# Threshold attention into a squared-ReLU feed-forward: the first batch in two parts, a maximum per head, and the sums' transposes between the value products

## The chip, the cores and the metric

The kernel runs on one NeuronCore of a Trainium2 chip. The metric is device microseconds of one execution. Every execution listed here was fast: within 1.5% of the fastest of its kernel. Where a run was timed against the kernel before, both ran alternately on the same chip. Different jobs ran on different chips, and the kernel before then had medians of 1672.2 to 1674.6 us; so kernels of different jobs are compared by their ratios to it. A ratio is the mean time of one kernel's fast runs over that of the other's in the same rounds, so it is not quite the ratio of the medians quoted.

## The reference

```python
batch, n_heads, seq, head_dim = (8, 8, 576, 64)      # q, k, v; float32
scores = (1 / sqrt(64)) * q @ k.T
thresh = max(scores) - tau                            # tau = 0.02
scores = where(scores >= thresh, scores, -1e9)
attn   = exp(scores - max(scores)); attn /= sum(attn) + 1e-9
x = (attn @ v) as (4608 tokens, 512)
out = relu(x @ w_in) ** 2 @ w_out                     # w_in 512 x 2048, w_out 2048 x 512
```

The weights come as float64. The kernel reads each number as two 32-bit words and makes a float32 of them.

## The kernel before

Two heads are handled together (a pair). A batch has four pairs. Queries go in five blocks per pair: four of 128 rows and one of 64, in which both heads share the partitions. So a batch has 20 blocks, called slots here, and eight batches have 160. All instructions on TensorE stand in the order in which the program emits them; on the other engines a scheduler orders them when the program is built. DVE, ACT and GpSimd take their instructions strictly in that order, as the Trainium skill's page "TensorE: Matmul & The Clock Gate" says (Part 1, on queue depths).

One slot: scores on TensorE into PSUM, softmax on DVE and ACT, transposes of the weights `w` on TensorE.

```python
def softmax(i, t, sc):                       # (cut)
    every = ...                              # both heads, 2 x 576 columns
    nc.vector.tensor_reduce(out=nmx[:, 0:nj], in_=every, axis=AXIS.X, op=ALU.max, negate=True)
    nc.vector.tensor_scalar(out=thr[:, 0:nj], in0=nmx[:, 0:nj], ...)
    for j in range(nj):
        nc.scalar.activation(out=w[:, ts(j, S)], in_=sc[...], func=AF.Exp, bias=nmx[:, j : j + 1])
    for j in range(nj):
        nc.vector.scalar_tensor_tensor(out=w[...], in0=sc[...], scalar=thr[:, j : j + 1], in1=w[...],
            op0=ALU.is_ge, op1=ALU.mult, accum_out=sm[...])
```

After a pair's five blocks come its value products. From the second batch on, the transposes of the reciprocal sums stand behind the products:

```python
    pv = [bank([P, n], "pv") for _, n in parts]          # 512 and 64 queries
    ...                                                  # products of v with the weights
    if b > 0:
        reciprocals()     # transposes pr, copy rb on ACT, transpose prr, copies rb on ACT
    for (q0, n), to in zip(parts, pv):
        ...  nc.vector.tensor_mul(xs[piece][...], to[...], rb[...])
```

The four banks of `bank()` (two in the first batch) serve all of these, the transposes and the feed-forward. A piece of feed-forward is 256 tokens: 64 products with `w_in` (out `ph`), 32 with `w_out` (out `po`). Its matmuls are put between the scores and the transposes of later slots, so that TensorE has work while softmax runs. In the first batch there are no finished tokens yet, so there is nothing to put in.

The weights are converted from the first slot on, 1.25 of 32 chunks per slot; in the trace 27 fall in the first batch and 5 in the second. One chunk passes through three engines:

```python
    nc.scalar.activation(out=a, in_=hi, func=AF.Abs)                            # L120
    nc.gpsimd.tensor_scalar(out=a, in0=a, ..., op0=ALU.min, op1=ALU.max)        # L122, the clamp
    nc.vector.tensor_scalar(out=t, in0=a, ..., shift and mask)                  # L126
    nc.vector.scalar_tensor_tensor(out=t, in0=hi, ..., in1=t)                   # L130
    nc.scalar.activation(out=r, in_=lo, func=AF.Copy, scale=2.0**-29)           # L134
    nc.gpsimd.tensor_tensor(out=dst, in0=t, in1=r, op=ALU.add)                  # L135
```

## Time and profile before

The median is 1674.5 us (1674.1 to 1674.6).

| stretch (us) | what runs | TensorE busy | granted clock | DVE busy | ACT busy |
|---|---|---|---|---|---|
| 9 to 136 | first batch, no feed-forward | 78% | 0.79 | 74% | 68% |
| 136 to 322 | second batch and feed-forward | 99% | 0.99 | 39% | 39% |
| 322 to 1502 | six batches and feed-forward | 99% | 1.00 | 34% | 35% |
| 1502 to 1673 | feed-forward alone | 97% | 1.00 | 1% | 11% |

A busy TensorE at a clock of 0.79 does less in the same time: both columns have to be read together. The conversion, which becomes important below, is seen in the groups of instructions with the shapes kept apart (line, engine, operation, shapes and count, then busy us and mean ns, then idle time of the engine before them and what ended it):

```profile
L126 DVE TENSOR_SCALAR t<-a 128x512 int32<-128x512 int32 x32 | 17.7, 554 | 22.3 <-POOL a L122 22.3
```

DVE stood 22.3 us for GpSimd's clamp in the whole run.

```profile
DVE t L126 <- POOL a L122: 7.7, 9, 2.6
```

### The profile page before, as it was taken

How to read it: one execution, taken by the hardware profiler on the slowest of the kernel's cores; microseconds unless marked ns; L12 is line 12 of the kernel's file. 1: busy time of each engine (PE TensorE's matmuls, PEld its weight loads, DVE VectorE, ACT ScalarE, POOL GpSimd, SP SyncE). 2: the span in 40 equal slices, each digit the busy share in tenths (PEclk: the TensorE clock that was granted, in tenths of full speed). 3: DMA queues.
4: the chain of work that ended last, by engine and by line, in shares of the span. 5: the costliest groups of instructions: out<-in, count | busy, mean ns of one | idle time of the engine just before them, and what ended most of it. 6: DMA issues, size and time to landing. Idle time of an engine off the chain costs nothing.

```text
span 1673.3 us, 19432 instructions
## 1 busy us (share of the span) xinstructions
PE 1616.4 (97%) x7616; PEld 1034.6 (62%) x7616; DVE 568.9 (34%) x1210; ACT 589.0 (35%) x1237; POOL 255.5 (15%) x296
## 2 busy tenths in 40 slices
PE   6879999999999999999999999999999999999998
PEld 3446666575756566575666665758575665756764
DVE  5784433333433333322223233333333333320000
ACT  5774433343433333332323333334333333321100
POOL 3451201020101101010110110102010110102211
PEclk7888999999999999999999999999999999999999
DMA  6551110101010010100000001010110000000000
GB/s 170 157 172 41 35 34 22 34 16 32 23 28 21 21 28 22 34 15 20 23 27 20 22 22 34 22 29 21 28 28 20 23 21 13 1 13 7 7 13 13
DMA packets 98347, 55.79 MB, mean 33 GB/s; under 512 B 83664, under 2 KB 91856, under 8 KB 98256
## 3 DMA queue, kind: packets, MB, share of 16 engines
q1 hardware_dynamic: 95376, 45.11, 10.3%
q0 software_dynamic: 2880, 9.44, 1.5%
q8 instruction: 61, 1.00, 0.2%
q14 instruction: 30, 0.25, 0.0%
HBM read 45.09 MB, written 9.44 MB: 33 GB/s over the span
## 4 chain that ended last, share of the span: by engine, by line
PE 91%; issue 3%; ACT 2%; DVE 2%; POOL 1%; DMA 1%; SPq 1%; POOLq 0%; ACTq 0%
PE ph L367 30%; PE po L382 29%; PE sc L233 11%; PE pv L343 7%; PE pwT L284 6%; PE pqk L194 2%; PE pv L337 2%; PE pr L324 1%; ACT rb L325 1%; PE pwR L294 1%; PE pwT L289 1%; DVE w L263 1%; DMA raw<-in_moe_w_in_dram 1%; ACT w L259 1%; DVE t L130 0%
## 5 line engine op out<-in xcount | busy, mean ns | idle before, releaser
L367 PE MATMUL ph<-x,w_in 128*128 128x256 f32 x2304 | 515.9, 381 | 5.1 <-ACT rb L325 5.1
L382 PE MATMUL po<-w_out,g 128*128 128x512 f32 x1152 | 512.3, 597 | 7.9 <-ACT rb L325 7.9
L367 PEld LDWEIGHTS ph<-x,w_in 128*128 128x128 f32 x2304 | 432.2, 190 | 69.4 <-ACT rb L325 7.3
L251 DVE TENSOR_REDUCE nmx<-sc 128x2 f32<-128x1152 f32 (+1 forms) x160 | 197.9, 1237 | 688.8 <-PE sc L233 677.4
L382 PEld LDWEIGHTS po<-w_out,g 128*128 128x128 f32 x1152 | 213.2, 190 | 254.5 <-issue 240.1
L263 DVE SCALAR_TENSOR_TENSOR w<-sc,thr,w 128x576 f32<-128x576 f32 x288 | 225.0, 815 | 134.8 <-ACT w L259 134.8
L259 ACT ACTIVATE w<-sc,nmx 128x576 f32<-128x576 f32 x288 | 200.0, 743 | 148.1 <-DVE nmx L251 146.6
L285 ACT COPY wT<-pwT 128x512 f32<-128x512 f32 x256 | 138.4, 589 | 316.5 <-PE pwT L284 316.3
L375 POOL TENSOR_TENSOR g<-h 128x512 f32<-128x512 f32 x144 | 149.9, 1041 | 566.6 <-ACT h L373 566.6
L233 PE MATMUL sc<-kT,qT 64*128 64x512 f32 (+3 forms) x1216 | 212.7, 467 | 1.1 <-DVE kT L199 1.1
L373 ACT ACTIVATE h<-ph 128x512 f32<-128x512 f32 x144 | 86.1, 598 | 277.6 <-PE ph L367 276.8
L233 PEld LDWEIGHTS sc<-kT,qT 64*128 64x128 f32 (+1 forms) x1216 | 100.0, 180 | 102.6 <-issue 90.7
L284 PEld LDWEIGHTS pwT<-ident,w 128*128 128x128 f32 x1024 | 121.5, 143 | 57.0 <-issue 32.2
L284 PE MATMUL pwT<-ident,w 128*128 128x128 f32 x1024 | 138.6, 279 | 18.2 <-DVE w L263 15.9
L343 PE MATMUL pv<-wT,va 128*64 128x64 f32 (+1 forms) x1024 | 131.8, 410 | 0.0
L343 PEld LDWEIGHTS pv<-wT,va 128*64 128x64 f32 x1024 | 54.3, 137 | 75.3 <-issue 73.1
L387 POOL DMA_DIRECT2D out_dram<-o x36 | 20.4, 566 | 523.0 <-ACT o L386 523.0
L386 ACT COPY o<-po 128x512 f32<-128x512 f32 x36 | 21.1, 586 | 188.5 <-PE po L382 188.5
L316 POOL COPY rx<-rcp 128x512 f32<-128x512 f32 x32 | 19.5, 609 | 249.8 <-DVE rcp L314 249.8
L356 DVE TENSOR_TENSOR x<-pv,rb 128x64 f32<-128x64 f32 (+3 forms) x120 | 30.3, 309 | 66.7 <-ACT rb L325 65.8
L325 ACT COPY rb<-pr 128x512 f32<-128x512 f32 x32 | 18.8, 586 | 89.8 <-PE pr L324 87.2
L294 PE MATMUL pwR<-ident,w 128*128 128x128 f32 x160 | 46.0, 288 | 4.0 <-ACT wT L285 4.0
(49 smaller groups left out, 667.8 us busy)
## 6 DMA issues: line engine op xcount, KB each, us to landing
out_dram<-o POOLq DMA_DIRECT2D x36, 256.0 KB, 2.3
qn<-in_q_dram SPq DMA_DIRECT2D x64, 128.0 KB, 2.6
kn<-in_k_dram SPq DMA_DIRECT2D x64, 128.0 KB, 2.9
va<-in_v_dram SPq DMA_DIRECT2D x32, 256.0 KB, 2.7
raw<-in_moe_w_in_dram SPq DMA_DIRECT2D x16, 512.0 KB, 4.7
raw<-in_moe_w_out_dram SPq DMA_DIRECT2D x16, 512.0 KB, 4.1
rn<-in_q_dram SPq DMA_DIRECT2D x32, 32.0 KB, 2.4
rn<-in_k_dram SPq DMA_DIRECT2D x32, 32.0 KB, 2.5
```

What stands on the lines that cost most here:

```text
L233: nc.tensor.matmul(to, qT[rows, ds(t * P, m)], kT[rows, ds(k0, n)], start=True, stop=True)
L251: nc.vector.tensor_reduce(out=nmx[:, 0:nj], in_=every, axis=AXIS.X, op=ALU.max, negate=True)
L259: nc.scalar.activation(out=w[:, ts(j, S)], in_=sc[:, ds(at[j], S)], func=AF.Exp, bias=nmx[:, j : j + 1], scale=1.0)
L263: nc.vector.scalar_tensor_tensor(out=w[:, ts(j, S)], in0=sc[:, ds(at[j], S)], scalar=thr[:, j : j + 1], in1=w[:, ts(j, S)], op0=ALU.is_ge, ...
L284: nc.tensor.transpose(pt[:, c, :], w[:, ds(j * (S + REST) + c * P, P)], ident[:, :])
L285: nc.scalar.copy(wT[:, j, :, ts(t, P)], pt[:, :, :])
L294: nc.tensor.transpose(pt[:, :], w[:, ds(MAIN, P)], ident[:, :])
L343: nc.tensor.matmul(to[rows, :], va[:, j, c, :], wT[:, j, c, ds(q0, n)], start=False, stop=(c == FULL - 1), skip_group_check=True,)
L367: nc.tensor.matmul(ph[:, m, :], w_in[:, c, ts(f + m, P)], x[:, c, :], start=(c == 0), stop=(c == NP - 1))
L373: nc.scalar.activation(out=h[:, :, :], in_=ph[:, :, :], func=AF.Relu)
L375: nc.gpsimd.tensor_mul(g[:, :, :], h[:, :, :], h[:, :, :])
L382: nc.tensor.matmul(po[:, :], gT[f][:, ts(s, P)], w_out[:, f, :], start=(f == 0), stop=(f == NF - 1))
```

## The change

Three things at once. The first batch goes in two parts: blocks 0 and 1 of all four pairs (8 slots), then blocks 2 to 4 of each (12 slots). After the first part 256 tokens are complete, so feed-forward can stand in the 12 slots and in the whole second batch. The conversions go at one chunk per slot in the first 8 slots and at two in the next 12. The slots of the second part also take over what the kernel before had only from slot 20 on: one score buffer of four banks in place of two of three banks, four shared banks in place of two, and scores that are issued only after the transposes of the slot before. The maximum is taken per head, so that the first head's exp can start sooner. The sums' transposes stand between the value products.

```diff
-        nc.vector.tensor_reduce(out=nmx[:, 0:nj], in_=every, axis=AXIS.X, op=ALU.max, negate=True)
+        for j in range(nj):
+            nc.vector.tensor_reduce(
+                out=nmx[:, j : j + 1], in_=sc[:, ds(at[j], S)], axis=AXIS.X, op=ALU.max, negate=True
+            )
 ...
-    def values(i):
+    def values(i, t0, t1):
 ...
-        if b > 0:
-            reciprocals()
+        pr = bank([P, FULL, P], "pr")
+        for t in range(nt):
+            nc.tensor.transpose(pr[:, t, :], rx[:, t, :, :].rearrange("p j d -> p (j d)"), ident[:, :])
+        nc.scalar.copy(rb[:, ds(t0 * P, nt * P)], pr[:, 0:nt, :].rearrange("p t m -> p (t m)"))
+        products(0)
+        if t1 == NB:
+            ...                       # prr and its copies
+            products(1)
 ...
-    slots = [(i, t) for i in range(len(pairs)) for t in range(NB)]
+    HALF = PT // P
+    slots = [(i, t) for i in range(NP) for t in range(HALF)]
+    slots += [(i, t) for i in range(NP) for t in range(HALF, NB)]
+    slots += [(i, t) for i in range(NP, len(pairs)) for t in range(NB)]
 ...
-        weights_until(min((5 * (n + 1)) // 4, len(chunks)))
+        weights_until(min(n + 1 + max(n + 1 - n_first, 0), len(chunks)))
 ...
-            late = min(run(per_slot * share[t] + late), 0.0)
+            late = min(run(per_slot * (0.25 if with_values else 4.75 / (NB - 1)) + late), 0.0)
```

(Left out: more buffers for `va`, `qT`, `kT`, the base of `per_slot`, and where the turns, that is the transposes of q and k, and the loads of the pairs stand. `share` was 0.5 in a slot with value products and 4.5/4 in the others.)

More of the change, by code (lines that the diff above doesn't have):

```diff
@@ L169, in load @@
         kn = sb.tile([P, FULL, P], FP32, tag="kn", name="kn")
-        va = sb.tile([P, 2, FULL, D], FP32, tag="va", bufs=3, name="va")
+        va = sb.tile([P, 2, FULL, D], FP32, tag="va", bufs=4, name="va")
         rn = sb.tile([P, P], FP32, tag="rn", name="rn")
@@ L188, in turn @@
         qn, kn, rn, va, vd = loaded.pop(i)
-        qT = sb.tile([P, S], FP32, tag="qT", name="qT")
-        kT = sb.tile([P, S], FP32, tag="kT", name="kT")
+        qT = sb.tile([P, S], FP32, tag="qT", bufs=4, name="qT")
+        kT = sb.tile([P, S], FP32, tag="kT", bufs=4, name="kT")
         for nat, to in ((qn, qT), (kn, kT)):
@@ L247, in softmax @@
         nmx = sb.tile([P, 2], FP32, tag="nmx", bufs=3, name="nmx")
-        every = sc[:, 0:S]
-        if nj == 2:
-            every = bass.AP(tensor=every.tensor, offset=every.offset, ap=[every.ap[0], [at[1], 2], [1, S]])
-        nc.vector.tensor_reduce(out=nmx[:, 0:nj], in_=every, axis=AXIS.X, op=ALU.max, negate=True)
+        for j in range(nj):
+            nc.vector.tensor_reduce(
+                out=nmx[:, j : j + 1], in_=sc[:, ds(at[j], S)], axis=AXIS.X, op=ALU.max, negate=True
+            )
         thr = sb.tile([P, 2], FP32, tag="thr", bufs=3, name="thr")
@@ L300, in transposes @@
                 nc.scalar.copy(wR[rows, rest], pt[rows, ds(j * REST, REST)])
-    def values(i):
+    def values(i, t0, t1):
         b, hp = pairs[i]
         wT, wR = weights.pop(i)
-        _, _, va, vd = turned.pop(i)
+        _, _, va, vd = turned[i]
         sm = sums.pop(i)
         last = 2 * FULL
+        nt = min(t1, FULL) - t0
+        s0, s1 = 2 * t0, min(2 * t1, last + 1)
         rcp = sb.tile([P, 2 * NB], FP32, tag="rcp", name="rcp")
-        nc.vector.tensor_scalar(
-            out=rcp[:, 0 : last + 1], in0=sm[:, 0 : last + 1], scalar1=1e-9, scalar2=None, op0=ALU.add
-        )
-        nc.vector.reciprocal(out=rcp[:, 0 : last + 1], in_=rcp[:, 0 : last + 1])
+        nc.vector.tensor_scalar(out=rcp[:, s0:s1], in0=sm[:, s0:s1], scalar1=1e-9, scalar2=None, op0=ALU.add)
+        nc.vector.reciprocal(out=rcp[:, s0:s1], in_=rcp[:, s0:s1])
         rx = sb.tile([P, FULL, 2, D], FP32, tag="rx", bufs=1, name="rx")
         nc.gpsimd.tensor_copy(
-            out=rx.rearrange("p t j d -> p (t j) d"), in_=rcp[:, 0:last].unsqueeze(2).broadcast_to([P, last, D])
+            out=rx[:, 0:nt, :, :].rearrange("p t j d -> p (t j) d"),
+            in_=rcp[:, s0 : s0 + 2 * nt].unsqueeze(2).broadcast_to([P, 2 * nt, D]),
         )
@@ L320, in values, with products @@
         yield
-        def reciprocals():
-            pr = bank([P, FULL, P], "pr")
-            for t in range(FULL):
-                nc.tensor.transpose(pr[:, t, :], rx[:, t, :, :].rearrange("p j d -> p (j d)"), ident[:, :])
-            nc.scalar.copy(rb[:, 0:MAIN], pr.rearrange("p t m -> p (t m)"))
+        parts = [(t0 * P, nt * P)] + ([(MAIN, REST)] if t1 == NB else [])
+        pv = [bank([P, n], "pv") for _, n in parts]
+        def products(which):
+            q0, n = parts[which]
+            for c in range(FULL):
+                for j in range(2):
+                    rows = ds(j * D, D)
+                    nc.tensor.matmul(
+                        pv[which][rows, :], va[:, j, c, :], wT[:, j, c, ds(q0, n)], start=False,
+                        stop=(c == FULL - 1), skip_group_check=True,
+                    )
+        for (q0, n), to in zip(parts, pv):
+            nc.tensor.matmul(to[:, :], vd[:, :], wR[:, ds(q0, n)], start=True, stop=False, skip_group_check=True)
+        pr = bank([P, FULL, P], "pr")
[4 more added lines that the diff above has]
+        if t1 == NB:
+            turned.pop(i)
             pr = bank([P, P], "prr")
@@ L330, in reciprocals @@
                 nc.scalar.copy(rb[rows, MAIN:S], pr[rows, ds(j * REST, REST)])
-        if b == 0:
-            reciprocals()
-        parts = [(0, MAIN), (MAIN, REST)]
-        pv = [bank([P, n], "pv") for _, n in parts]
-        for (q0, n), to in zip(parts, pv):
-            nc.tensor.matmul(to[:, :], vd[:, :], wR[:, ds(q0, n)], start=True, stop=False, skip_group_check=True)
-        for (q0, n), to in zip(parts, pv):
-            for c in range(FULL):
-                for j in range(2):
-                    rows = ds(j * D, D)
-                    nc.tensor.matmul(
-                        to[rows, :], va[:, j, c, :], wT[:, j, c, ds(q0, n)], start=False, stop=(c == FULL - 1),
-                        skip_group_check=True,
-                    )
-        if b > 0:
-            reciprocals()
+            products(1)
         for (q0, n), to in zip(parts, pv):
@@ L410, in run @@
         return us
-    slots = [(i, t) for i in range(len(pairs)) for t in range(NB)]
-    n_first = NP * NB
-    share = [0.5] + [4.5 / (NB - 1)] * (NB - 1)
+    HALF = PT // P
+    slots = [(i, t) for i in range(NP) for t in range(HALF)]
+    slots += [(i, t) for i in range(NP) for t in range(HALF, NB)]
+    slots += [(i, t) for i in range(NP, len(pairs)) for t in range(NB)]
+    n_first, n_batch = NP * HALF, NP * NB
+    ends = {}
+    for i in range(len(pairs)):
+        ends[i, NB - 1] = (HALF if i < NP else 0, NB)
+        if i < NP:
+            ends[i, HALF - 1] = (0, HALF)
     due = deque()
@@ L420, in begin, with values_due @@
         softmax(i, t, scores(i, t))
-        if due:
-            for _ in due.popleft():
-                pass
-            b, hp = pairs[i - 1]
-            if hp == NP - 1:
-                feed_forward_until((b + 1) * S)
+        return values_due()
+    def values_due():
+        if not due:
+            return False
+        i, t1, job = due.popleft()
+        for _ in job:
+            pass
+        b, hp = pairs[i]
+        if hp == NP - 1:
+            feed_forward_until(b * S + min(t1 * P, S))
+        if i < 2 and t1 == NB:
+            load(NP + i)
+        return True
     def prepare(n):
         i, t = slots[n]
-        if t == NB - 2 and i + 1 < len(pairs):
+        if (t == 0 and i + 1 < NP) or (t == NB - 2 and NP <= i + 1 < len(pairs)):
             turn(i + 1)
-            if i + 2 < len(pairs):
+            if i + 2 < NP or NP + 2 <= i + 2 < len(pairs):
                 load(i + 2)
@@ L438, in end @@
         transposes(i, t)
-        if t == NB - 1:
-            job = values(i)
+        if (i, t) in ends:
+            t0, t1 = ends[i, t]
+            job = values(i, t0, t1)
             next(job)
-            due.append(job)
+            due.append((i, t1, job))
     def convert_for(n):
-        weights_until(min((5 * (n + 1)) // 4, len(chunks)))
+        weights_until(min(n + 1 + max(n + 1 - n_first, 0), len(chunks)))
     with ExitStack() as stack, tc.manual_schedule(engines={mybir.EngineType.PE}):
@@ L453 @@
         for n in range(n_first):
+            prepare(n)
             if n + 1 < n_first:
@@ L456 @@
             end(n)
-            prepare(n)
             convert_for(n)
@@ L462 @@
         for n in range(n_first, len(slots)):
-            t = slots[n][1]
-            begin(n)
+            with_values = begin(n)
             prepare(n)
             convert_for(n)
-            if n % n_first == 0:
-                per_slot = asked["us"] / n_first
-            late = min(run(per_slot * share[t] + late), 0.0)
+            if n == n_first:
+                per_slot = 2 * asked["us"] / (2 * n_batch - n_first)
+            elif n % n_batch == 0:
+                per_slot = asked["us"] / n_batch
+            late = min(run(per_slot * (0.25 if with_values else 4.75 / (NB - 1)) + late), 0.0)
             end(n)
-        for _ in due.popleft():
-            pass
-        feed_forward_until(B * S)
+        values_due()
         run(float("inf"))
```

## The prediction

> **What bounds the kernel now.** I read the stretches first, then TensorE's waits in each stretch, then single places in the timeline. The page gives PE 97% busy. The stretches (columns: PE, weight loads, DVE, ACT, POOL, granted clock, DMA) show where the other part lies. The first batch's 20 blocks begin their scores at 9.1 us, the second's at 136.0, the third's at 323.1 (timeline of PE).
>
> ```profile
> core 0: us, PE busy (x) PEld busy (x) DVE busy (x) ACT busy (x) POOL busy (x), PEclk, DMA share, GB/s
> 9.00:136.00 127.00, 98.60 (x454) 53.48 (x453) 94.42 (x191) 86.64 (x174) 57.93 (x66) 0.79 0.55 161
> 322.00:508.00 186.00, 183.62 (x909) 118.51 (x908) 67.06 (x144) 67.25 (x144) 21.25 (x24) 1.00 0.10 25
> ```
>
> The reader is to see that the first batch is the only bad stretch: PE idles 28 of 127 us there, and its clock is 0.79. From the second batch to 1502 us PE is 99% busy at full clock, with DVE and ACT at 36%. The last 171 us are feed-forward alone. What the first batch should cost PE follows from a later pair of heads: from the start of its value products at 464.20 to those of the next at 510.70 are 46.5 us, of which 64 matmuls of po at 0.429 us (64 in 27.47 us on the chain) are 27.5 and one wait is 0.6, so attention is 18.4 us a pair and 74 us a batch. The first batch takes 127: 53 us of it are idleness and a slow clock.
>
> TensorE's waits, first 0 to 136 us, then 168 to 1502 us:
>
> ```profile
> PE pwT L284 <- DVE w L263: 15.9, 12, 2.2
> PE pqk L194 <- DMA qn<-in_q_dram: 4.6, 1, 4.6
> PE pwR L294 <- ACT wT L285: 4.0, 7, 2.4
> ```
>
> ```profile
> PE po L382 <- ACT rb L325: 7.9, 14, 0.6
> PE ph L367 <- ACT rb L325: 4.5, 8, 0.6
> PE prr L327 <- ACT rb L325: 3.4, 5, 0.7
> ```
>
> In the first batch PE waits for softmax, since no feed-forward exists yet to put in between. Later there is one repeating wait, 27 times, 15.8 us in all: the copy of the reciprocal sums. The timeline shows one:
>
> ```profile
> 469.97 0.27 PE L327 MATMUL prr<-ident,rcp 128*128 128x128 f32 x1
> 470.17 0.59 ACT L325 COPY rb<-pr 128x512 f32<-128x512 f32 x1 [3.08 <-PE pr L324]
> ...
> 470.81 3.70 PE L382 MATMUL po<-w_out,g 128*128 128x512 f32 x8 [0.57 <-ACT rb L325]
> ```
>
> With pv twice, pr and prr, the four shared PSUM banks are out, and the next user stands until the copy has freed pr's.
>
> **What the Trainium skill says.** "Perfetto Trace Analysis", Optimization Strategy: where the most contended engine changes over time, interleaving the regimes can help. That is the main part of this change, and the table above agrees that there are two regimes. The same page, Matmuls: groups should rotate through banks so that the evacuation of one overlaps the next group's matmuls; the 0.57 us wait is this not happening. The same page, Optimizing Scalar/DVE Operations: each DVE instruction pays a fixed cost, about 125 ns on PSUM, and breaking instructions up may let work end sooner where DVE only causes bubbles. The trace gives 1357 ns for the maximum of both heads and 757 for 576 columns, so 157 ns for the split. "TensorE: Matmul & The Clock Gate", Part 1: the array runs at half clock until it has been busy for about 3.4 us, and again after an idle window. The trace fits: eight transposes took this long at 16 us and at 53 us, and the 10 us stretches of the first batch lie between 0.53 and 1.00.
>
> ```profile
> 16.18 1.92 PE L284 MATMUL pwT<-ident,w 128*128 128x128 f32 x8 [2.18 <-DVE w L263]
> 53.31 1.06 PE L284 MATMUL pwT<-ident,w 128*128 128x128 f32 x8 [0.56 <-DVE x L356]
> ```
>
> **The change, part by part.** The order of PE's instructions in the changed kernel gives the counts. Blocks 0 and 1 of all four pairs of the first batch come first (8 slots), then blocks 2 to 4 of each (12 slots), then as before. After 8 slots one piece of 256 tokens is complete, and its feed-forward is placed into the 12 slots: 64 products with w_in and 10 with w_out. At 0.436 (128 instructions, so 64 products, in 27.89 us) and 0.858 us they are 27.9 + 8.6 = 36.5 us. That leaves slots 20 to 40, where PE is the bound, so these get 36.5 us shorter. No PE work is removed, and splitting the value products by columns keeps their total width. The gain is 36.5 us less what slots 0 to 20 get longer.
>
> *Slots 0 to 7.* All four turns of q and k now fall into 8 slots, and one weight conversion per slot instead of 1.25. DVE per two slots: four maxima at 0.757 = 3.0, thresholds 0.5, four masks at 0.815 and their accumulator reads 0.083 = 3.6, kT 0.7, reciprocals 0.35, x 0.4, two conversions at 0.554 + 0.761 = 2.6: 11.2 us. Before, DVE was 74% busy here (94.4 of 127); at that share it is 15.1 us a pair. TensorE: 98.6 / 4 = 24.7 us a pair before; two blocks with a turn and a half product are about half of that, 12.3, which at its old share of 78% makes 15.8. The head-wise maximum takes some 0.4 us off each block's latency (exp of the first head starts 0.6 us earlier, the threshold 0.16 later), so I choose 14 us: 56 in all, and the first block of the second part at 65 us.
>
> *Slots 8 to 19.* The rest of the 32 weight conversions, two per slot, fall here, together with the feed-forward. Demand per pair (three slots):
>
> - TensorE at full clock: scores 3.6, transposes 2.8, products and sums 3.2 (the warm spans of later blocks, cut to 320 columns), 21 products with w_in 9.2: 18.8 us.
> - ACT: five exp at 0.743 = 3.7, weights' copies 4.1, sums 0.8, six conversions at 0.687 + 0.688 = 8.3, 2.7 ReLU at 0.598 = 1.6: 18.5 us.
> - DVE: five maxima 3.8, thresholds 0.7, five masks with reads 4.5, six conversions 7.9, the rest 1.3: 18.2 us.
>
> So three engines want about 6.2 us a slot at once, with one score buffer (four banks, one deep) between them. They can't all be full. DVE's best 10 us stretches before were 91 to 93% busy, its mean 74%; I choose 86%, which makes 21.8 us a pair and 87 for the twelve slots, at nearly full clock. The second batch then begins at 152 instead of 136.
>
> *The sums' transposes.* pr now comes before the value products, so its copy of 0.59 us lies beside 3.5 us of matmuls, and prr takes a freed bank. The 15.8 us of later waits should go. One pv, one pv, one pr and one accumulating bank of the feed-forward are just four, so nothing new has to wait.
>
> *The maximum per head* after slot 20: 0.157 us more DVE on some 110 blocks, 17 us of work on an engine 36% busy; nothing on the path.
>
> *Sum:* 36.5 - 16 = 20.5 for the interleaving, 16 for the sums (15.8, rounded): 36.5 us. 1674.5 - 36.5 = 1638 us.
>
> **Rivals.**
>
> 1. The conversions become the bound in slots 8 to 19. For it: the rows of three engines just added; three buffers for raw weights, 512 KB each, 4 to 5 us to landing; and the conversion shares 12 buffers with the feed-forward's squares, of which one piece holds 8, leaving 4 for a conversion that wants 3. ACT and DVE then wait in order, and softmax behind them. Against it: in slots 20 to 25 before, conversions ran beside the feed-forward and PE stayed 100% busy (though at 9.3 us a slot). If a slot takes 8.8 us, the twelve take 105, the gain falls to 18 us: 1656.
> 2. The slots get to TensorE's bound: 75 us for the twelve and 52 for the eight, because dense matmuls keep the clock up. Then the second batch starts as early as before, all 36.5 us are gained, and with the sums it is 53: 1621. For it: demand of PE is the largest of the three. Against it: how evenly they stand.
> 3. The sums' wait is only replaced by another, x's multiplication holding both pv banks while DVE finishes the block's masks. Against it: prr's bank comes free first, and 0.9 us of feed-forward already under way still stands in between. It would cost up to 16 us: 1654.
>
> **Range and chances.** The two sure quantities are the 36.5 us moved and the 15.8 us of waits; uncertain is the length of the first 20 slots, 141 to 165 us at their end, and a few us of the waits. That makes 1624 to 1656. The border of 2% is 1641, three us above my number, so faster by over 2% is only somewhat likelier than within: 0.57 to 0.41. Slower would need slots 8 to 19 at over 12 us each: 0.02.
>
> **What would show it.** In the changed profile: the first feed-forward matmul near 68 us instead of 144.6; the second batch's scores near 152; the clock near 1.0 from there back to about 70 us; the third batch's scores near 300 instead of 323; no wait of po, ph or prr on rb beyond 2 us in sum; 288 maxima of about 757 ns; later pairs of heads 46 instead of 46.5 us. The prediction is wrong if PE's waits on DVE's w, on ACT or on the weights' landing exceed some 15 us between 65 and 152 us, or if a wait on x replaces that on rb.

## More of the kernel before

```profile
DVE t L126 <- POOL a L122: 14.6, 4, 5.7
```

So only a third of it was in the first batch. The longer waits stood beside feed-forward, where TensorE stayed busy.

## The result and the profile after

The changed kernel takes 1652.6 us median (1652.2 to 1654.3), the kernel before 1674.6 in the same rounds: ratio 0.987, with a 95% interval of 0.9853 to 0.9887. It is faster by 1.3%, within the predicted range (1624 to 1656) and near its slow end, 14.6 us above the number named.

The stretches, with the columns of the first fence in the prediction:

```profile
9.00:64.00 55.00, 43.17 (x207) 24.39 (x206) 39.67 (x89) 36.14 (x73) 21.95 (x32) 0.85 0.69 183
64.00:169.00 105.00, 94.62 (x487) 62.18 (x485) 61.89 (x138) 60.83 (x124) 50.53 (x57) 0.87 0.36 114
320.00:507.00 187.00, 187.00 (x935) 119.46 (x930) 69.06 (x168) 67.21 (x146) 21.29 (x24) 1.00 0.10 25
```

The first 8 slots end near 64 us, as expected. The next 12 take until 169 instead of 152, with a clock of 0.87. No engine but TensorE is more than 59% busy there. Later TensorE is never idle.

Where the time went is told by a mark that both kernels have: the start of the last transpose of a slot (pwR in the timeline of TensorE). The profiled execution of the changed kernel was the slowest of its four (1654.3 us).

| | before | after | difference |
|---|---|---|---|
| until the end of slot 19 | 135.6 | 168.7 | +33.1 |
| slots 20 to 39 | 187.3 | 145.8 | -41.5 |
| slots 40 to 159 | 1172.3 | 1160.4 | -11.9 |
| the rest | 178.1 | 177.6 | -0.5 |
| span | 1673.3 | 1652.5 | -20.8 |

TensorE's waits between 66.3 and 168.7 us (slots 8 to 19) in the changed kernel, then DVE's in the same stretch (who waited for whom, us in total, times, longest):

```profile
PE pwT L284 <- DVE w L263: 6.4, 5, 4.0
PE po L384 <- DVE x L358: 1.8, 1, 1.8
PE pwT L289 <- DVE w L263: 1.2, 2, 0.9
```

```profile
DVE t L126 <- POOL a L122: 21.8, 17, 3.0
DVE nmx L249 <- PE sc L233: 10.7, 6, 3.3
```

DVE stands longest not for scores but for GpSimd's clamp. What that does is seen in slot 11, the first with the value products of a second part (blocks 2 to 4 of a pair) (timeline, all engines, cut):

```profile
89.82 1.30 PE L233 MATMUL sc<-kT,qT 64*128 64x512 f32 x8
...
91.65 0.69 DVE L130 SCALAR_TENSOR_TENSOR t<-raw,t 128x512 int32<-128x512 int32 x1
...
92.50 1.27 POOL L135 TENSOR_TENSOR w_in<-t,r 128x512 int32<-128x512 int32 x1 [1.16 <-DVE t L130]
93.74 0.61 POOL L122 TENSOR_SCALAR a<-a 128x512 f32<-128x512 f32 x1
...
94.38 0.43 DVE L126 TENSOR_SCALAR t<-a 128x512 int32<-128x512 int32 x1 [2.04 <-POOL a L122]
...
94.84 0.69 DVE L130 SCALAR_TENSOR_TENSOR t<-raw,t 128x512 int32<-128x512 int32 x1
95.45 1.42 DVE L249 TENSOR_REDUCE nmx<-sc 128x1 f32<-128x576 f32 x2
...
99.93 0.87 PE L284 MATMUL pwT<-ident,w 128*128 128x128 f32 x3 [3.98 <-DVE w L263]
```

The scores are there at 91.1 us. DVE's next instructions are two conversions, the second of which needs GpSimd's clamp, and that stands in GpSimd's own queue behind the addition of the chunk before, which needs DVE. The maximum gets its turn at 95.45, 4.3 us late; for 2.04 us of these DVE stood for the clamp. TensorE has only value products and two products of feed-forward in such a slot, runs out at 95.9 and stands 3.98 us. And then it is slow (columns as above):

```profile
97.00:99.00 2.00, 0.00 (x0) 0.00 (x0) 1.44 (x5) 1.96 (x5) 0.66 (x2) 0.96 0.60 225
99.00:101.00 2.00, 1.07 (x5) 1.08 (x6) 1.91 (x7) 0.27 (x1) 1.71 (x2) 0.50 0.58 143
103.00:105.00 2.00, 2.00 (x10) 1.25 (x7) 0.54 (x1) 0.00 (x0) 0.60 (x1) 0.50 0.75 250
105.00:107.00 2.00, 2.00 (x9) 1.74 (x8) 1.11 (x3) 1.40 (x3) 0.66 (x1) 0.83 0.03 12
```

The granted clock is 0.50 when work resumes and returns between 105 and 107 us, some 6 us later. In slots 8 to 19 the granted clock was 0.50 in four stretches, 25.9 us in all: 66.3 to 75.0, 98.8 to 105.7, 126.2 to 129.6 and 150.0 to 156.9. The last three each follow a wait in a slot with value products (4.0, 1.9 and 1.8 us). The first began at 61.3 us, still in slot 7, so 8.7 of the 25.9 us were carried over from the first part.

The sums' part shows as it should (timeline of all engines, slot 11): the copy lies beside the products, and no wait is named at prr.

```profile
91.75 0.39 PE L340 MATMUL pr<-ident,rx 128*128 128x128 f32 x2
92.07 1.95 PE L331 MATMUL pv<-wT,va 128*64 128x256 f32 x16
92.22 0.37 ACT L341 COPY rb<-pr 128x256 f32<-128x256 f32 x1
93.94 0.32 PE L346 MATMUL prr<-ident,rcp 128*128 128x128 f32 x1
```

Between 168.7 and 1480 us the list of TensorE's waits is empty.

### The profile page after: what moved, and what is told of

Same layout as the page of the kernel before. It is cut to its first block, busy times and chain, and to the rows that moved or that the text cites. A ratio compares the mean times of both kernels' runs of the same rounds, so it can differ in the third digit from the quotient of the medians.

```text
span 1652.5 us, 19839 instructions
## 1 busy us (share of the span) xinstructions
PE 1618.2 (98%) x7704; PEld 1034.4 (63%) x7704; DVE 569.8 (34%) x1346; ACT 586.2 (35%) x1241; POOL 252.9 (15%) x300
## 3 DMA queue, kind: packets, MB, share of 16 engines
q1 hardware_dynamic: 95376, 45.11, 10.4%
## 4 chain that ended last, share of the span: by engine, by line
PE 91%; issue 3%; DVE 2%; POOL 2%; ACT 2%; DMA 0%; SPq 0%; POOLq 0%; ACTq 0%; DVEq 0%
PE ph L369 29%; PE po L384 28%; PE sc L233 11%; PE pv L331 8%; PE pwT L284 7%; PE pv L337 2%; PE pqk L194 2%; PE pwR L294 1%; PE pr L340 1%; PE pwT L289 1%; ACT w L259 1%; DVE nmx L249 1%; DVE t L130 1%; DVE w L263 0%; POOL a L122 0%
## 5 line engine op out<-in xcount | busy, mean ns | idle before, releaser
L249 DVE TENSOR_REDUCE nmx<-sc 128x1 f32<-128x576 f32 x288 | 206.4, 753 | 680.9 <-PE sc L233 675.2
L233 PE MATMUL sc<-kT,qT 64*128 64x64 f32 (+3 forms) x1248 | 211.5, 454 | 0.0
L284 PE MATMUL pwT<-ident,w 128*128 128x128 f32 x1024 | 137.9, 277 | 13.1 <-DVE w L263 11.3
L331 PE MATMUL pv<-wT,va 128*64 128x64 f32 (+2 forms) x1088 | 142.7, 405 | 0.0
L316 POOL COPY rx<-rcp 128x512 f32<-128x512 f32 (+1 forms) x36 | 20.3, 564 | 264.7 <-DVE rcp L314 264.5
L337 PE MATMUL pv<-wR,vdiag 128*128 128x64 f32 (+2 forms) x136 | 43.8, 442 | 0.1
L341 ACT COPY rb<-pr 128x512 f32<-128x512 f32 (+1 forms) x36 | 19.4, 538 | 64.1 <-PE pr L340 64.1
```

The lines of the kernel that those rows point to most:

```text
L233: nc.tensor.matmul(to, qT[rows, ds(t * P, m)], kT[rows, ds(k0, n)], start=True, stop=True)
L249: nc.vector.tensor_reduce(out=nmx[:, j : j + 1], in_=sc[:, ds(at[j], S)], axis=AXIS.X, op=ALU.max, negate=True)
L284: nc.tensor.transpose(pt[:, c, :], w[:, ds(j * (S + REST) + c * P, P)], ident[:, :])
L331: nc.tensor.matmul(pv[which][rows, :], va[:, j, c, :], wT[:, j, c, ds(q0, n)], start=False, stop=(c == FULL - 1), skip_group_check=True,)
L337: nc.tensor.matmul(to[:, :], vd[:, :], wR[:, ds(q0, n)], start=True, stop=False, skip_group_check=True)
```

## The experiments

The theory: the sums' part gives its gain in full; the interleaving loses part of its gain in slots 8 to 19, because conversions that wait for GpSimd stand in DVE's queue ahead of the maximum, whereupon TensorE idles and then runs on a slow clock. The rivals: three engines are simply full there, or the single score buffer and the slow clock alone set these slots. The first four runs take out or keep single parts (the interleaving alone was not run), the next four test the conversion, the last four try to mend it. Edits are shown as code or, where that is long, summed up in words.

### e1_sums_only: the sums' part alone

```diff
  kernel before, from the second batch on:
-        products of both parts; reciprocals()
+        pr and its copy; products(0); prr and its copies; products(1)
```

> The kernel before with only the sums' transposes moved between the value products, from the second batch on. If the 15.8 us of waits on rb were on the path and nothing replaces them: 1674.6 - 16 = 1658 to 1659 us (ratio 0.990 to 0.991), and TensorE waits on rb below 1 us between 168 and 1502 us. If the wait is only replaced by one on x's multiplication (rival 3 of the prediction): 1670 us or more, with such waits in the trace.

Measured: 1660.2 us (1656.4 to 1661.4), the kernel before 1672.2 on that chip; ratio 0.9926 (0.9910 to 0.9943), so about 12 us. There is no wait of TensorE between 168 and 1490 us. Slots 40 to 159 take 1160.4 us in its trace, to the tenth what the changed kernel takes, against 1172.3 before. The part is worth what its waits were, less a few us, and no other wait of TensorE took their place.

### e2_max_only: the maximum per head alone

```diff
  kernel before:
-        one tensor_reduce over both heads
+        one tensor_reduce per head
```

> The kernel before with only the maximum taken per head. My theory: 0.16 us more DVE per block is beside the path after the first batch, and in the first batch the threshold comes 0.16 us later but the first exp 0.6 us earlier: between -4 and +1 us, so 1670 to 1675. The rival that DVE's extra work counts in the first batch, where DVE is 74% busy: 16 blocks of two heads at 0.157 us = 2.5 us more, 1677.

Measured: 1677.5 us (1675.9 to 1678.3) against 1672.2; ratio 1.0033 (1.0018 to 1.0048). My theory of a gain in the first batch fell: the edit costs 3 to 8 us. The group shows the added work, 206.3 us where before had 197.9 (173.7 and 24.2):

```profile
L249 DVE TENSOR_REDUCE nmx<-sc 128x1 f32<-128x576 f32 x288 | 206.3, 753 | 684.7 <-PE sc L233 675.1 <-PE sc L237 9.5
```

In its trace slot 19 ends at 137.7 instead of 135.6, and TensorE's waits on `w` are 19.7 us instead of 15.9. The rival's 2.5 us of added DVE work in the first batch is about this size. What else the split changes in the order of DVE's queue I did not follow.

### e3_after_one_max: the changed kernel with one maximum

```diff
  changed kernel:
-        one tensor_reduce per head
+        one tensor_reduce over both heads
```

> The changed kernel with one maximum for both heads again. If the head-wise maximum shortens the softmax chain in the first 20 slots: 1653 to 1657. If it was only more DVE work: 1649 to 1652. Either way the twelve slots from 64 to 169 us stay above 95 us, because I lay their length to the weight conversions in DVE's queue.

Measured: 1649.4 us (1648.9 to 1649.7); ratio 0.9865 (0.9851 to 0.9880). The ratio is not told apart from the changed kernel's 0.987. It does not show the gain that I had hoped for from the head-wise maximum. Slots 8 to 19 take 98.5 us in its trace instead of 102.4, still above 95; e4 below shows that traces of the same instructions differ by nearly as much.

### e4_after_sums_last: the changed kernel with the sums behind the products

```diff
+        if b > 0:
+            products(0)
+            products(1)
         pr = bank([P, FULL, P], "pr")
         ...                              # and no products after pr and prr where b > 0
```

> The changed kernel with the sums' transposes after the value products again, from the second batch on. If this part alone gave the 17 us that the changed kernel gains after the first 20 slots: 1652.6 + 16 = 1668 to 1670, with some 15 us of TensorE's waits on rb. If the gain there is something else, for instance the shorter feed-forward in the value slots: under 1660.

Measured: 1665.6 us (1658.5 to 1668.0, a wide spread); ratio 0.9953 (0.9924 to 0.9983). By the ratios about 14 us of the changed kernel's gain are gone, a little less than expected. The waits are back (between 168 and 1490 us):

```profile
PE ph L374 <- ACT rb L344: 7.4, 13, 0.6
PE po L389 <- ACT rb L344: 6.8, 12, 0.6
PE prr L350 <- ACT rb L344: 1.4, 2, 0.7
```

Slots 40 to 159 take 1172.0 us. With e1 this settles the sums' part. What e4 keeps of the change, interleaving and head-wise maximum, is worth 8 us (3 to 13), where the prediction had 20.5. Its first 20 slots have the changed kernel's instructions in the same order, and its slots 8 to 19 take 99.6 us where that trace has 102.4: a difference of 3 us there between two traces says nothing.

### e5_after_clamp_dve: the clamp on DVE

```diff
-        nc.gpsimd.tensor_scalar(
+        nc.vector.tensor_scalar(
             out=a[:, :], in0=a[:, :], scalar1=as_float(high), scalar2=as_float(low), op0=ALU.min, op1=ALU.max
         )
```

> The changed kernel with the clamp of the weight conversion on DVE instead of GpSimd, so that a conversion no longer goes ACT, GpSimd, DVE, GpSimd and DVE's queue never stands for GpSimd's clamp. My theory: the slots 8 to 19 took 105 us instead of 87 because conversions that wait for GpSimd stand in DVE's queue ahead of the block's maximum, PE then idles up to 4 us and runs at half clock for some 8 us after it. Then slots 8 to 19 fall to 80 to 92 us and the time to 1630 to 1642, though DVE has 0.5 us more work per conversion. Rival: three engines are simply full (DVE, ACT and PE about 6.2 us a slot): then DVE's added 16 us make it slower, 1655 to 1668.

Measured: 1643.6 us (1641.7 to 1643.9); ratio 0.9816 (0.9802 to 0.9831): faster than the changed kernel's 0.987 by half a per cent, 9 us. Slots 8 to 19 take 92.2 us (columns of the stretches, here from the end of slot 7 to that of slot 19; the changed kernel first, then this one):

```profile
66.30:168.70 102.40, 92.02 (x481) 61.54 (x481) 60.49 (x134) 59.03 (x119) 48.97 (x54) 0.87 0.36 112
```

```profile
63.90:156.10 92.20, 84.01 (x484) 56.21 (x483) 79.45 (x158) 60.16 (x122) 39.46 (x34) 0.97 0.40 129
```

DVE is busy 19 us longer, and the stretch is 10.2 us shorter: 8.0 us in TensorE's busy time and 2.2 in its idle time. That rules out the rival that DVE's work was the bound. The size is less sure: the traces differ by 12.6 us in all and the ratios by 9, as the profiled execution was the fastest of its four here (1641.7 us) and the slowest there. The clock was at 0.50 for 6.4 us of the stretch instead of 25.9; about 3 us of the gain (an estimate, half of 8.7 less 2.9 us) belong to the slow stretch that slot 7 leaves behind. DVE's masks (0.81 us each) and maxima (0.75) took as long in both kernels, so the clamp on GpSimd had not slowed them. The edit also shortens GpSimd's own queue, which no run separates from DVE's wait. DVE's wait for GpSimd, 21.8 us, is gone:

```profile
DVE nmx L249 <- PE sc L233: 4.3, 3, 2.2
DVE w L263 <- ACT w L259: 3.5, 5, 1.2
DVE a L122 <- ACT a L120: 3.2, 4, 1.0
```

Both the length and the time lie just above what I had expected (80 to 92, and 1630 to 1642). Some conversions still stand ahead of maxima, and TensorE still waits 8.2 us in the stretch (10.4 before this edit).

### e6_before_clamp_dve: the control

```diff
  kernel before:
-        nc.gpsimd.tensor_scalar(      # the clamp
+        nc.vector.tensor_scalar(
```

> Control: the same edit in the kernel before. Its first batch waited for softmax too, with DVE 74% busy. If GpSimd in the conversion's chain is what stands in DVE's queue there as well: 5 to 12 us faster, 1662 to 1670. If the first batch of the kernel before is bound by DVE's work itself: same or up to 10 us slower.

Measured: 1674.8 us (1674.2 to 1675.3); ratio 1.0005 (0.9990 to 1.0020): the same. DVE is then 105.0 us busy of 126.5 in the first batch, and TensorE still waits 16.8 us on `w`. The clock rose from 0.79 to 0.88 and TensorE's busy time fell from 98.2 to 93.9 us, but it waited for softmax instead. I read it so: without feed-forward to put in, softmax on DVE binds that stretch, and taking a wait from DVE's queue while adding work to it gains nothing. No run shows this; it also counts that there was less to take away, 7.7 us of DVE's waits for the clamp against 21.8 in slots 8 to 19 of the changed kernel.

### e7_after_cheap and e8_before_cheap: hardly any conversion

```diff
-        ...  Abs, clamp, shift and mask, merge, low word, addition
+        nc.scalar.activation(out=dst, in_=hi.bitcast(FP32), func=AF.Copy)
```

The result is wrong: the weights are nonsense. Loads, matmuls and slots stay.

> The changed kernel with the weight conversion cut to one copy on ACT per chunk (wrong result on purpose: the weights are nonsense), so no conversion on DVE or GpSimd. If the conversions lengthen the slots 8 to 19: these take 76 to 84 us and the time is 1610 to 1630 (the first eight slots get shorter too). If the single score buffer or PE's slow clock alone sets these slots: they stay above 95 us and the time above 1640.

> Control, wrong on purpose in the same way: the kernel before with the conversion cut to one copy on ACT. If conversions also set much of its first batch: 1640 to 1655. If its first batch is set by softmax alone: 1665 or more. The difference between this and the changed kernel with the same cut shows what the interleaving is worth without conversions: by the prediction's sum 36.5 us less what it adds, plus 16 for the sums, so 30 to 50 us.

Measured: the changed kernel 1629.6 us (1628.4 to 1630.0), ratio 0.9733; the kernel before 1664.2 us (1663.5 to 1667.6), ratio 0.9946. So the conversions cost the kernel before 9 to 10 us and the changed one 23. Slots 8 to 19, from 59.5 to 144.2 us:

```profile
59.50:144.20 84.70, 80.69 (x483) 56.17 (x483) 38.48 (x92) 45.74 (x96) 10.09 (x13) 0.98 0.40 123
```

This is 84.7 us at a clock of 0.98, with the same single score buffer. The rival that buffer and clock alone set these slots is out: the clock recovers once the conversions are gone. The length is just above what I expected. For e8 neither expectation was met (1640 to 1655, or 1665 and more), and the second came close: its first batch still takes 117.6 us, so most of that length is not the conversions'. The difference of the two, 34.6 us, is what the whole change is worth where no conversion is in the way.

### e9_even_share: feed-forward evenly over slots 8 to 19

```diff
+            share = 0.25 if with_values else 4.75 / (NB - 1)
+            if n < n_batch:
+                share = 0.875
```

> The changed kernel with the feed-forward spread evenly over slots 8 to 19 (7 products with w_in in every slot) instead of 2 in a value slot and 9 or 10 in the others. My theory: PE's idle time in value slots (4.0, 1.9 and 1.8 us, DVE's maximum behind the conversions) both costs itself and drops the clock (0.87 over these slots). With 5 more products (2.2 us) standing there, the idle time of value slots falls below 3 us in all, the clock rises above 0.93 and slots 8 to 19 take 90 to 96 us instead of 102: 1640 to 1647. Rival: softmax then lags in the other slots, whose cover falls from 4.4 to 3.1 us, by as much: 1650 to 1658.

Measured: 1647.3 us (1644.7 to 1649.7); ratio 0.9832 (0.9816 to 0.9849). Slots 8 to 19 take 97.2 us at a clock of 0.92:

```profile
66.60:163.80 97.20, 87.44 (x479) 57.93 (x479) 61.49 (x133) 58.17 (x119) 49.25 (x54) 0.92 0.38 119
```

Between both expectations. The idle time of the slots with value products fell below 1 us, as expected, but in all it is 9.8 us, hardly less than 10.4, because slots without value products (9, 12, 15 and 18) now run out of cover, as the rival had it. But the single waits are shorter (2.9 us at most, not 4.0), and TensorE's busy time fell by 4.6 us for the same matmuls: more of them ran on the full clock.

### e10, e11, e12: combinations

e10 is the clamp on DVE with one maximum for both heads; e11 adds the even share; e12 instead converts 1.6 chunks per slot in all 20 slots.

```diff
  e10, e11, e12: the edits of e5 and e3
  e11 also: the edit of e9
  e12 also:
-        weights_until(min(n + 1 + max(n + 1 - n_first, 0), len(chunks)))
+        weights_until(min((8 * (n + 1)) // 5, len(chunks)))
```

> The changed kernel with the clamp on DVE and one maximum for both heads: one wait and 0.16 us of DVE per block fewer. If the maximum per head costs in the first 20 slots, as it did in the kernel before (5 us) and as the run of the changed kernel without it hints (3 us): 2 to 5 us below the run with the clamp alone, 1638 to 1642. If the head-wise maximum helps once DVE no longer waits for GpSimd: 1644 to 1647.

> Both of these edits and the even share together. If the two mend the same idle time: about the better of the two alone, 1637 to 1642. If they add up: 1630 to 1636, with slots 8 to 19 near 80 us.

> Clamp on DVE, one maximum, and the conversions spread evenly over the first 20 slots (1.6 per slot) instead of 1 per slot in the first 8 and 2 in the next 12. If what counts is conversions beside feed-forward in slots 8 to 19: these get shorter by 3 to 6 us, the first 8 longer by 2 to 4: 1636 to 1641. If the first 8 slots are as sensitive: the same or up to 5 us slower than without this edit.

| | median (range), us | ratio (95%) | end of slot 7 | end of slot 19 | slots 8 to 19 |
|---|---|---|---|---|---|
| e10 | 1639.6 (1637.2 to 1640.7) | 0.9790 (0.9775 to 0.9804) | 61.5 | 153.9 | 92.4 |
| e11 | 1640.4 (1637.7 to 1642.3) | 0.9795 (0.9781 to 0.9810) | 63.6 | 156.7 | 93.1 |
| e12 | 1642.1 (1641.2 to 1644.9) | 0.9809 (0.9795 to 0.9824) | 64.5 | 157.0 | 92.5 |

e10 has the lowest time of the kernels that give correct results, though e11 is not told apart from it. It beats both the kernel before and the changed kernel. Whether it is over 2% faster than the kernel before stays unclear, as its interval reaches 0.9804. Against e5 (0.9816, the intervals just overlap) its gain lies in the first 8 slots, which end 2.4 us earlier with one maximum; slots 8 to 19 are as long. The even share adds nothing to it: TensorE is idle for 9.3 us of slots 8 to 19 in e11 and for 8.1 in e10. The even rate of conversions makes the first 8 slots 3.0 us longer and the next 12 no shorter, so between 1.6 and 2 per slot it is not the number of conversions beside the feed-forward that counts.

What I could not try: the maximum put ahead of the conversions in DVE's queue with everything else kept. I built a kernel that emits no conversions in slots with value products, but the scheduler left two of them ahead of the maximum all the same, so I did not run it. That the place in the queue matters, and not only the wait inside the conversion, is therefore read from the timeline of slot 11 and not shown by a run.

## Why the prediction was right, and where it was not

The time fell within the range, and the result within 2%, to which I had given 0.41 against 0.57 for more. That the range held is owed to its width, which reached as far as the first rival's 1656 us; the number itself was 14.6 us off, two fifths of the predicted gain. The sum was 36.5 us, the medians show 22.0, the trace 20.8. Its terms, one by one:

- **The feed-forward moved out of slots 20 to 40.** 36.5 us and its share of the sums predicted; these slots are 41.5 us shorter. 2 us belong to the sums (one batch of the six that follow gains 2.0). Of the other 3, an estimated 2 are the clock: the kernel before ran the first 3.9 us of its second batch at a granted clock of 0.50, and in e8, where the clock was 1.00 there, that batch takes 185.5 us instead of 187.3.
- **The sums' transposes.** 15.8 us of waits, 16 predicted. Slots 40 to 159 gained 11.9 and one batch more 2, so 14 us in the trace, and 12 to 14 us in e1 and e4. The mechanism holds, the size was a little too high.
- **Slots 0 to 7.** Predicted to end at 65 us; the scores of slot 8 start at 64.3.
- **Slots 8 to 19.** This is the step that failed: "They can't all be full. DVE's best 10 us stretches before were 91 to 93% busy, its mean 74%; I choose 86%, which makes 21.8 us a pair and 87 for the twelve slots, at nearly full clock." They took 102.4 us. The 86% was laid on TensorE's 18.8 us a pair, so the 87 us held 75 us of TensorE's work and 12 of idle time. The idle time came out at 10.4 us, which the share hit without a reason for it. What failed is "at nearly full clock": TensorE was busy for 92.0 us, at 0.87. In e7 the same matmuls took 80.7 us at 0.98, with 4.0 us idle; so of the 17.7 us by which the conversions lengthen these slots, 11.3 are TensorE's busy time, by the slower clock, and 6.4 its idle time. TensorE's 75 us were also too few, as e7 shows; they left out the turn of the second batch's first pair (1.1 us in e7). For DVE and ACT the demand was too high: they were 60.5 and 59.0 us busy, where four times 18.2 and 18.5 would be 73 and 74, as 21 conversions and not 24 fell there. So neither was full, and yet the slots were longer. A share of busy time, which I used, has no term for short waits that drop the clock.
- **The maximum per head.** I had counted it as a help in the first slots ("takes some 0.4 us off each block's latency") and nothing later. It is nothing later (slots 40 to 159 take 1172.3 us with it in e2, as before), but in the kernel before it costs 3 to 8 us by e2, and e10 against e5 hints at 2.4 us in the first 8 slots.

Of the rivals, the first came out to a few us: it had 105 us for the slots and 1656 in all. Its reason was half right. The conversions are the cause, as e7 shows, but no run or row shows the engines full, and of waits that may be for the twelve buffers there are under 2 us (ACT for GpSimd's addition). What I had not seen is that a conversion waits, on its way through GpSimd, inside the queue that softmax needs. The profile before had a hint, though not the size: DVE's waits for the clamp, 7.7 us in the first batch and, beside feed-forward in the second, up to 5.7 us at once. The second rival, that TensorE's bound is reached, needed the conversions gone: e7's 84.7 us is closest. The third, a wait on x in place of that on rb, did not come: e1 shows none after the first batch, and the changed kernel one of 1.8 us, in slot 17.

My list of signs also had a gap. I had put 15 us of waits between 65 and 152 us as the mark of failure; there were 9, of them 7 on `w` and ACT. The slow clock was on the list, but I had not put a price on it, and it was the larger part. The first feed-forward matmul was to come near 68 us and came at 74.2.

## What to carry to other kernels

Before moving work into a stretch, follow each side job (here a dtype conversion) through all the queues it passes: where it goes back and forth between two engines, the queue of the engine that waits stands still, and that can delay a chain that has nothing to do with it although every engine shows spare time. Count a wait on TensorE together with the slow clock that follows it; here the clock was the larger part. What only has to get out of PSUM again, like the reciprocal sums here, goes ahead of the long products, beside which TensorE had no wait for its copy in e1.

## What the Trainium skill lacked or had wrong

- "TensorE: Matmul & The Clock Gate": Part 1 gives about 3.4 us of sustained activity for the clock to return, in a window that runs freely, and lets the moment vary by 0.5 us. After the 4.0 us wait of slot 11 TensorE worked again from 99.9 us on at a granted clock of 0.50, which came back between 105 and 107 us, so it took about 6 us of work, of which the first 2 us were transposes. Part 4 says that the full clock does not engage in transpose mode. Transposes here, which the profile names MATMUL without telling the mode, ran at both speeds: eight took 1.92 us at 16 us and 1.06 us at 53 us. Whether they count as activity for the gate no run here tells.
- "Perfetto Trace Analysis", Optimization Strategy, advises to interleave regimes. It lacks the condition: a side job that is interleaved must not wait inside a queue that the other regime needs. Without conversions the change was worth 34.6 us (e7 against e8), with them 22.
- The same page, Optimizing Scalar/DVE Operations, says that breaking up instructions may let work be completed sooner where DVE only causes bubbles. It may not: here one maximum made into two cost about 0.15 us of DVE a block (1357 ns before, 753 twice in e2) and, by e2, 0.33% of the whole time.
